# The first tile of a scan's coefficients normalised in four parts instead of two, under a newly searched written order

## Chip, cores and metric

One Trainium2 chip, one core. The time is microseconds (us) on the device for one execution of the program, from the host's data in the chip's main memory to the result there. Layout work on the host (permuting, padding, viewing the weights as 64-bit words) lies outside the time.

## What is computed

A gated linear attention with complex decay, and behind it one feed-forward layer (`moe`). Per batch, head and time step the decays are limited in magnitude, a 48x48 complex state is decayed and receives an outer product, and the query reads its real part:

```python
mag = np.sqrt(a_re * a_re + a_im * a_im)
scale = np.minimum(mag, 0.999) / (mag + 1e-06)
ar, ai = a_re * scale, a_im * scale            # "a normalised"
for t in range(768):                            # B=4, H=8, S=768, D=48
    new_re = ar[t] * S_re - ai[t] * S_im
    new_im = ar[t] * S_im + ai[t] * S_re
    S_re, S_im = new_re + outer(k[t], v[t]), new_im
    y[t] = q[t] @ S_re
h = y.reshape(3072, 384) @ w_in                 # 384 x 2048
out = (h * clip(h + 3, 0, 6) / 6) @ w_out       # 2048 x 384
```

## The kernel before

Time is cut into 24 chunks of 128 steps (`NCH`), each with a batch; two batches take turns. Three chunks at a time share one tile of coefficients: eight tiles, called q0 to q7 here, each with a `z` tile of 128 partitions x 2 (real, imaginary) x 18 rows x 68 columns, where the 18 rows are two halves `f` (time running backward and forward from the middle of a chunk) of nine rows.

The work is written as 13 streams, Python generators that each issue a few instructions between two `yield`s (a step). A string `ORDER` of letters says which stream makes its next step. The string is the program's order on every engine: TensorE (PE), VectorE (DVE), ScalarE (ACT), GpSimd (POOL) and the DMA queue of SyncE (SP) each run their own instructions strictly in the order in which they were written, and wait on one another by semaphores alone. The streams that matter here, with their letters:

- `load` (Z): one DMA of one part of a `z` tile. A tile is loaded into the place of the tile two before it, so q2's load waits until `prep` of chunk 2 has read q0 for the last time.
- `normal` (N for even, O for odd parts): normalises one part in four steps. Step 1 is ACT Square (its sum goes to a column of `accs`), an add of the two halves (DVE for q0, POOL for all later tiles) and ACT Ln; step 2 is two ACT Exp and a multiply (again DVE for q0, POOL later); step 3 one DVE instruction and an ACT Copy; step 4 one DVE instruction and the multiplication of the part itself (two DVE instructions of one plane each in half 0, one of both planes in half 1). Its scratch tile `sq` has two buffers, `y2` one. How a tile is cut into parts stands in `PARTS`: at most nine rows, so two parts for each tile.
- `chain` (C): running products over a whole tile on DVE, when all parts of it are normalised: seven steps, three steps e0 to e2 (written `pr`, `z`), six wide instructions of 882 elements, and at the end a few POOL instructions and six small DMAs (`cw`).
- `prep` (Q for chunk 1, P for the others): loads `u` and `gg`, then on ACT, DVE (POOL from q2 on) makes reciprocals of the products and multiplies q and k with them (`gg`, four products), and transposes through six DMAs `kq<-gg`; last a load of `vt`.
- `load_weights` (D) loads one of 16 blocks of both weight matrices (`ws`, four buffers); `weights` (W) turns the 64-bit words into numbers in two steps: ACT and one DVE instruction (L308), then two DVE, one ACT and one POOL instruction (L317).
- `mat` (A): the attention of one chunk: `pA` (PE), masked by DVE into `am`, `py`, transposes `pt` copied by ACT into `kn`, `pG` for the state, and the result `xh`, `xl`.
- `moe` (M): the feed-forward layer of three chunks at once, eight groups of 16 blocks: `ph` (PE), `r` (ACT), `hs` (DVE; from group 3 on `gh` and `gl`), `po` (PE). A group starts when its three chunks' `mat` steps are done.
- `weights_guard` (G), `wsplit` (S), `verdict` (V): checks of the weights' range, the splitting of `w_out` in two, and the final check of the inputs' ranges.

In the order before, the letters begin `ZNNZZZONQNOOOCNCCCCOCCCCCCOCCPDWPODDDWPQ`. Spelled out, with qT.i for part i of tile qT, up to the first feed-forward block:

```
load q0.0; normal q0.0 steps 1, 2; load q0.1, q1.0, q1.1; normal q0.1, q0.0, chunk 1's u, gg ... ;
chain q0 step 1; normal q1.0 step 1; chain q0 steps 2 to 5; normal q1.1 step 1; chain steps 6 .. e2, wide;
normal q1.1 step 2 (amid the wide ones); loads: chunk 0's u, gg, ws 0 to 3; weights 0; prep 0 (its six kq DMAs); ...
mat 0; weights 4, 5; (amid it) mat 1 pA; normal q1.0 steps 3, 4; weights 6 first step; prep 2 last products;
ws 7, 8, 9; weights 6, 7; prep 2 kq (3 DMAs); load q2.0; prep 2 kq (3); chain q1 step 1; ... weights 8;
normal q2.0 step 1; mat 1 py; load q2.1; mat 1 pt; vt of chunk 2; ws 10, 11; ... mat 1 pG, x; mat 2; moe block 0
```

## Time and profile before

| what | value |
|---|---|
| three runs | 712.55, 715.45, 721.03 us (median 715.45) |
| the profiled execution | 718.27 us, span of its instructions 716.5 us |
| PE busy | 593.6 us, 83% of the span |
| DVE busy | 510.7 us, 71% |
| ACT, POOL busy | 352.5 us, 175.9 us |
| granted TensorE clock, mean | 0.975 |

The 1.8 us between the span and the execution's time lie outside the first and last instruction. Busy PE is matmul time as modelled; the weight loads (PEld) overlap it. L12 is line 12 of the kernel.

Of the kernel before, what the change touches and what calls it, by code (L numbers as in the profile page):

```python
# [29 lines left out]

PAR = dict(
    PV=2, SZ='33333333', CS='3.3.3.3.3.3.3.3', GGB=1, SQB=2, ZB=2, XB=2, WTB=4, LAG=1, RB=2, OV=1, KQB=2,
    GS=3, VTB=2, IL=2
)

ORDER = (
    "ZNNZZZONQNOOOCNCCCCOCCCCCCOCCPDWPODDDWPQPPPPPPWWQWQWDQQQQPOANAPPWDAAACDWAAWWAAWNWNWPDDDWWPZPCWWCNAZA"
    "APDDWCWAAADACOAAACAACCACAMMCWMMMDCMMMMMCCCMMMWPMMMMMMMMMMMMPWPPMMMMMMMMWMDMMCMMWPPWMMMMMOWWPPMMMMMMM"
    "NMMMMOMWWMMMMDMMMAMMAMMPPMMMMANAAAPWPPMMPWNWMMMOPPPAAMMMMMMMMMMMMACPCMMMPGCPCGPGGGCCCCCMCMMMMMMMMPAA"
    "MGGZZCCCPAAAACOMMMMMMMMPPPMAAAMMMMMPPNAAAPPAPAAANMONAAPOMPMNMMMMMMOPMAAPMGMMMMMCMMMMPMMGPMMGGAAAACCC"  # L40
    "MMCPCMMMMMCCCGAMMMGMMMMPPPPGGAPPPMSSCAMMMMMMMAMMAMMMMGMMMMCCPCMGMAAPAAMMPPPPMMMMMMGMAMGMMMPMZZAAMMMM"
    "MMCNNPPAMAMMOMNMMAPOPMPMMMMMOMNOAMAMMMMMMPMMMMGMMMMMMMMMMAGAPCMMMMMPPCPAAAMMACMMMAACAACCCCMMGPMMMMMA"
    "MMPPPMMGGPGAMPPCCCMMMMMMMMMMMZAMAMASSCCNMMMMMMGNMMMPSMMPPSMMAPMMMMMPMASMSMMZGNSMPMMMMPPMMOMNAMSSMMMM"
    "MMPAASSSAOPMMMMMMAASPMMMMMPPMSAPAAAGPPPPPSMMMOMMOCMMMMMMMMMACCMMSSSSAMMMSSSMMMMMMCMPPMMMMGMCAMMPCPSG"
    "GAPMMCAMAMMAMMMZCPMCMMMMMCCPPPAAAMAACNNMMMMMMMMSMMMMMMMAAMMMMMMCCMMMMZPAMMMMMMMMMMMAMMMMAMMMMAMSPPMP"
    "MPOMMMSAAAMMMMPMPMMSMMMCMMMMMMMMOMMMMMMMMPPOANAMMSSMMMMMMMPMMPPMPPAOAAMMMAMSMMMMMMMMMAMNMMMMMPPMMMCA"
    "MPCMMMMAAACCMMMMMMMMMMMPMMMAPAAMMMMMMPMMMAMMMMCMMMMMMMMMMMMZCMMMMMMMMPCMCMNPCCMMMMMMMNMMAAAAMMMMAMPC"
    "MMMMMMZMAAAAMNCMCMMMPMMMMAMAPMMMMMMMCMPMMMMPPPPMMMMMAMMMMMMMMMMMMMMNOMOMMMPMMMMMAPAPMMMMMMMMAMMAMMMM"
    "MOMAMMPAMPAOPPPPPMMMMMMMMMAMMMMCCMMMMMPCCMMMMMMMAMAAMMMMMMMMMMMPPCMMMMMPPMMMMACAAAMMMCMMMMMCMAMMMMMM"
    "PMMMCCAAMAMCMMMMMMMMMGMAMMMPMAAACACPCMAPAMMMMPMMMMMMMMPPMPPMMMMMMMMMMMMMMMMMMMMMPAPMMMMMMMMAAMPPMMMM"  # L50
    "MMMMMMMMMMMMMAAMAMAMMMMMPMPPPMMMMMMMMMMMMMMMMMMMMMMMMMMMAMAPPPMMMMMMMMMMMMPMMMMMMMMMMMMMMMMPAAMMPMPM"
    "MAMMMMMMMMMMMMMMMPMMAAAMMMMMMMMMPAAAMMMMMMMMMMMMMMMMMAAMMMAAMMMMMMMMMMMMMMMMMMMMMMMMMMMMMMMMMMMMMMMM"
    "MMMMMMMMMMMMMMMMMMMMMVMMMMMMMMMMMMMMMMMMMMMMMMMMMMMMMMMMMMMMMMMMMMMMMMMMMMMMMMMMMMMMMMMMMMMMMMMMMVMM"
    "MM"
)
GGB, SQB, ZB, XB, WTB, LAG, RB, OV, KQB = (
    int(PAR[k]) for k in ("GGB", "SQB", "ZB", "XB", "WTB", "LAG", "RB", "OV", "KQB")
# [1 line left out]

GS, VTB = int(PAR["GS"]), int(PAR["VTB"])  # L60
PV = int(PAR.get("PV", 0))
# [2 lines left out]
SIZES = [int(x) for x in PAR.get("SZ", "222333333")]  # L64
NG, NCH = len(SIZES), B * S // C

IL, SEQ = int(PAR["IL"]), S // C
TURN = [(b + i) * SEQ + j for b in range(0, B, IL) for j in range(SEQ) for i in range(IL)]
FIRST = [sum(SIZES[:g]) for g in range(NG + 1)]
# [2 lines left out]
CHAINS, CHUNK, LAST = [], [], []  # L72
for _t, _ns in enumerate(PAR.get("CS", "3.3.3.3.3.3.3.3").split(".")):
# [3 lines left out]
    LAST.append(len(CHUNK) - 1)  # L77

PARTS = [
    [(f, x, min(9, 3 * n - x)) for f in range(2) for x in range(0, 3 * n, 9)] for _, n, _ in CHAINS  # L80
]
COLS = [sum(len(p) for p in PARTS[:q]) for q in range(len(CHAINS) + 1)]
MAXN = max(n for _, n, _ in CHAINS)
# [147 lines left out]
def tile_gated_attention_moe(ctx, tc, aL, GL, vL, wL, maskL, qkvaL, out):  # L231
# [66 lines left out]
    def weights(f):  # L298
# [10 lines left out]
        yield  # L309
        wout[f] = wp.tile([C, DM], F32, tag="wo", name="wo", bufs=NFF + (GS < NG))  # L310
        for part, bits in ((0, low[:, 0]), (1, wout[f].bitcast(I32))):
# [340 lines left out]
    def moe(g):  # L652
# [12 lines left out]

        split = g >= GS

# [57 lines left out]
    def wsplit(f):  # L725


        if "wl" not in LATE:
# [4 lines left out]
            LATE["wl"] = pl.tile([C, NFF, DM], F32R, name="wout_l")  # L733
        while f and GS and (GS - 1, f - 1) not in SECOND:
            yield "wait"
# [7 lines left out]
    def verdict():  # L743

        while len(NORMAL) < COLS[-1] or len(CWs) < len(CHAINS) or len(GUARDED) < 2 * NFF or "pg" not in LATE:
            yield "wait"
        ok = wp.tile([C, 8], F32, name="ok")
        P.memset(ok, 1.0)
        one = LATE["pg"].tile([C, DM], F32, tag="r", name="one", bufs=RB)
        for col, src, lim, op in (  # L750
            (0, accs[:, 0], SUM_M2_MAX, ALU.is_le),
            (1, accs[:, 1], SUM_Y_MAX, ALU.is_le),
            (2, n64, N64_MIN, ALU.is_ge),
            (3, wacc.rearrange("p a x -> p (a x)"), 1.0, ALU.is_le),
        ):
            p, n = src.shape
            t = one[:p, :n]
            V.tensor_scalar(t, src, lim, None, op)
            V.tensor_reduce(ok[:p, col : col + 1], t, mybir.AxisListType.X, ALU.min)
        okm = wp.tile([C, 1], F32, name="okm")  # L760
        V.tensor_reduce(okm, ok, mybir.AxisListType.X, ALU.min)
        yield
        pt = ps_a.tile([1, C], F32, tag="ps", name="pok")
        T.transpose(pt, okm, ident)
        okr = wp.tile([1, 1], F32, name="okr")
        V.tensor_reduce(okr, pt, mybir.AxisListType.X, ALU.min)
        V.tensor_copy(oki, okr)
        yield

    def each(make, items):  # L770
        for x in items:
            yield from make(*x)
# [15 lines left out]
        "D": each(load_weights, steps),  # L788
        "S": each(wsplit, steps if GS < NG else []),
        "V": verdict(),  # L790
# [117 lines left out]
```

### The profile page before, as it was taken

To read this page: it belongs to the slowest core of one execution; us is meant where nothing else is said; L and a number is where in the kernel's file an instruction comes from. 1 tells how busy PE (TensorE), PEld (TensorE's weight loads), DVE (VectorE), ACT (ScalarE), POOL (GpSimd) and SP (SyncE) were. 2 spreads that over 40 slices of the span, in tenths; PEclk is the share of its full clock that TensorE was granted. 3 is DMA by queue.
4 is the path that set the end of the run, shared out by engine and by line. 5 is a ranking of instruction groups with operands and counts; after the bars stand their busy time and mean duration, and the time that the engine had idled before them with its cause. 6 is when DMAs were issued, how large, how long until landed. Compare 5 with 4: busy or idle time off the path is not lost.

```text
span 716.5 us, 12111 instructions
## 1 busy us (share of the span) xinstructions
PE 593.6 (83%) x4433; PEld 521.7 (73%) x4433; DVE 510.7 (71%) x995; ACT 352.5 (49%) x721; POOL 175.9 (25%) x193
## 2 busy tenths in 40 slices
PE   0005359998568989989998999999999999999995
PEld 0004347776356767777777999999999998998995
DVE  3998857989858876787888657987688855453432
ACT  5334332565657776567646454444643443423332
POOL 0204230342143143315740333221302211300000
PEclk9999999999689999999999999999999999999998
DMA  9009872257746885476566234242453244140001
GB/s 344 23 18 206 253 211 78 67 121 163 183 102 161 194 225 96 127 179 157 104 126 150 80 72 79 86 70 90 82 126 45 82 82 78 50 60 34 1 0 38
DMA packets 55508, 79.61 MB, mean 111 GB/s; under 512 B 12432, under 2 KB 40208, under 8 KB 55440
## 3 DMA queue, kind: packets, MB, share of 16 engines
q1 hardware_dynamic: 55440, 78.75, 46.7%
q8 instruction: 37, 0.61, 0.4%
q14 instruction: 31, 0.25, 0.1%
HBM read 51.05 MB, written 4.72 MB: 78 GB/s over the span
## 4 chain that ended last, share of the span: by engine, by line
PE 38%; DMA 9%; DVE 8%; ACT 7%; issue 3%; POOL 3%; SPq 1%; ACTq 0%; DVEq 0%; POOLq 0%
PE ph L690 15%; PE po L673 5%; PE po L674 5%; PE po L675 5%; DMA kq<-gg 3%; PE py L585 3%; DMA out_dram<-ot 2%; DMA wgs<-in_wL_dram 2%; PE pA L569 2%; PE po L677 2%; PE pG L632 1%; ACT r L696 1%; DVE gg L528 1%; POOL gg L518 1%; DVE pr L408 1%
## 5 line engine op out<-in xcount | busy, mean ns | idle before, releaser
L696 ACT ACTIVATE r<-ph,half 128x384 f32<-128x384 f32 x128 | 73.7, 577 | 113.9 <-PE ph L690 109.4
L677 PE MATMUL po<-wo,hs 128*128 128x384 f32 x288 | 108.3, 509 | 16.7 <-DVE hs L708 16.7
L690 PE MATMUL ph<-xh,win_l 128*128 128x384 f32 x384 | 102.7, 376 | 2.8 <-ACT xh L647 2.8
L569 PE MATMUL pA<-kq 96*128 96x128 f32 x384 | 53.9, 296 | 61.2 <-DMA kq<-gg 59.3
L569 PEld LDWEIGHTS pA<-kq 96*128 96x128 f32 x384 | 51.7, 209 | 63.8 <-issue 61.4
L690 PE MATMUL ph<-xl,win_h 128*128 128x384 f32 x384 | 90.5, 344 | 1.0 <-DVE xl L648 1.0
L690 PE MATMUL ph<-xh,win_h 128*128 128x384 f32 x384 | 89.9, 342 | 0.0
L699 DVE SCALAR_TENSOR_TENSOR ph<-r,ph 128x384 f32<-128x384 f32 x80 | 44.8, 560 | 62.5 <-ACT r L696 62.3
L673 PE MATMUL po<-wh,gl 128*128 128x384 f32 x240 | 84.9, 354 | 4.2 <-DVE gl L704 3.8
L677 PEld LDWEIGHTS po<-wo,hs 128*128 128x128 f32 x288 | 53.9, 197 | 44.6 <-DVE hs L708 18.5
L674 PE MATMUL po<-wout_l,gh 128*128 128x384 f32 x240 | 81.9, 341 | 0.0
L675 PE MATMUL po<-wh,gh 128*128 128x384 f32 x240 | 81.0, 337 | 0.0
L690 PEld LDWEIGHTS ph<-xh,win_l 128*128 128x128 f32 x384 | 70.4, 192 | 14.4 <-ACT xh L647 2.9
L704 DVE TENSOR_TENSOR gl<-ph,gh 128x384 fp32r<-128x384 f32 x80 | 44.5, 557 | 41.0 <-ACT gh L702 40.9
L690 PEld LDWEIGHTS ph<-xl,win_h 128*128 128x128 f32 x384 | 69.4, 191 | 1.9 <-DVE xl L648 1.5
L690 PEld LDWEIGHTS ph<-xh,win_h 128*128 128x128 f32 x384 | 69.5, 190 | 0.6 <-issue 0.6
L702 ACT ACTIVATE gh<-ph 128x384 fp32r<-128x384 f32 x80 | 39.2, 490 | 60.9 <-DVE ph L699 60.9
L408 DVE TENSOR_TENSOR pr<-z 128x288 f32<-128x288 f32 (+2 forms) x176 | 66.6, 419 | 1.4
L518 POOL TENSOR_TENSOR gg<-gg,u 128x384 f32<-128x384 f32 x18 | 19.5, 1084 | 142.4 <-ACT u L516 126.7
L632 PE MATMUL pG<-vt,kn 128*96 128x64 f32 x320 | 34.9, 268 | 21.4 <-ACT kn L604 21.4
L673 PEld LDWEIGHTS po<-wh,gl 128*128 128x128 f32 x240 | 45.5, 189 | 8.4 <-DVE gl L704 7.3
L632 PEld LDWEIGHTS pG<-vt,kn 128*96 128x96 f32 x320 | 33.3, 183 | 24.6 <-ACT kn L604 22.1
(101 smaller groups left out, 1042.9 us busy)
## 6 DMA issues: line engine op xcount, KB each, us to landing
kq<-gg SPq DMA_DIRECT2D x138, 128.0 KB, 4.7
ws<-in_wL_dram SPq DMA_DIRECT2D x16, 768.0 KB, 7.2
wgs<-in_wL_dram SPq DMA_DIRECT2D x32, 384.0 KB, 3.8
z<-in_aL_dram SPq DMA_DIRECT2D x16, 612.0 KB, 5.5
vt<-in_vL_dram SPq DMA_DIRECT2D x24, 256.0 KB, 5.2
out_dram<-ot SPq DMA_DIRECT2D x24, 192.0 KB, 1.9
u<-in_GL_dram SPq DMA_DIRECT2D x23, 192.0 KB, 5.0
gg<-in_GL_dram SPq DMA_DIRECT2D x23, 192.0 KB, 2.6
```

The source lines that it names most:

```text
L408: V.tensor_tensor(pr[:, j], src, fac[:, j : j + 1].to_broadcast([C, *shape]), ALU.mult)
L569: T.matmul(pA[:, i], kt[:, hf * 4 + i], qt[:, hf * 4 + i], start=True, stop=True)
L632: T.matmul(pG[:, n], kn[:, n], vt[:, n], start=True, stop=True)
L673: T.matmul(po[i], gl[:, ts], wout_h[f], start=f == 0, stop=False)
L674: T.matmul(po[i], gh[:, ts], LATE["wl"][:, f], start=False, stop=False)
L675: T.matmul(po[i], gh[:, ts], wout_h[f], start=False, stop=f == NFF - 1)
L677: T.matmul(po[i], hs[0][:, ts], wout[f], start=f == 0, stop=f == NFF - 1)
L690: T.matmul(ph, w[:, f, kt * C : (kt + 1) * C], xx[:, kt], start=k == 0, stop=k == 8)
L696: A.activation(r, ph, AF.Relu, scale=1.0 / 6.0, bias=half)
L699: V.scalar_tensor_tensor(ph, r, 1.0, ph, ALU.min, ALU.mult)
L702: A.activation(gh, ph, AF.Copy)
L704: V.tensor_tensor(gl, ph, gh, ALU.subtract)
```

## The change

`PARTS` cuts tile q0 into parts of at most `R0` = 5 rows: per half one of five and one of four rows, four parts in place of two of nine (q1 to q7 keep nine). `accs` has 18 columns in place of 16, `load` makes 18 DMAs in place of 16, and `normal` has 18 parts in place of 16. The formulas, the tile of q0 and all else are the same. `ORDER` is a new string of 1,712 letters in place of 1,702.

```diff
 PAR = dict(
     PV=2, SZ='33333333', CS='3.3.3.3.3.3.3.3', GGB=1, SQB=2, ZB=2, XB=2, WTB=4, LAG=1, RB=2, OV=1, KQB=2,
-    GS=3, VTB=2, IL=2
+    GS=3, VTB=2, IL=2, R0=5
 )
 ORDER = (
-    "ZNNZZZONQNOOOCNCCCCOCCCCCCOCCPDWPODDDWPQPPPPPPWWQWQWDQQQQPOANAPPWDAAACDWAAWWAAWNWNWPDDDWWPZPCWWCNAZA"
-    "APDDWCWAAADACOAAACAACCACAMMCWMMMDCMMMMMCCCMMMWPMMMMMMMMMMMMPWPPMMMMMMMMWMDMMCMMWPPWMMMMMOWWPPMMMMMMM"
...
+    "ZZZZZNNZONNONOONONNDDDQOOPDOCCCCCCCCCCCCCWOOPWOPWPQPPPPWPQQWDDQNQWODANAWPQAAACWPAAPWWPWNZZWNWDDAANDW"
+    "CWCQWCWAPPAAWCPPAAADDAAOCWAAAADCCCAACWMMMMMCMMMMMCCDMMMMMMMMMMCMWMMPMMMMWPWDMMMMMMMMMMMMMMMCWWPPPMMM"
...
 )
+R0 = int(PAR["R0"])
 PARTS = [
-    [(f, x, min(9, 3 * n - x)) for f in range(2) for x in range(0, 3 * n, 9)] for _, n, _ in CHAINS
+    [(f, x, min(r, 3 * n - x)) for f in range(2) for x in range(0, 3 * n, r)]
+    for t, n, _ in CHAINS
+    for r in [9 if t else R0]
 ]
```

The new order spelled out up to the first feed-forward block:

```
load q0.0 to q0.3, q1.0; normal q0.0 steps 1, 2; load q1.1; normal q0.1 step 1, q0.0 steps 3, 4, q0.1 step 2,
q0.2 step 1, q0.1 steps 3, 4, q0.2 step 2, q0.3 step 1, q0.2 steps 3, 4; ws 0, 1, 2; chunk 1's u, gg;
q0.3 step 2, 3; chunk 0's u, gg; ws 3; q0.3 step 4; chain q0 whole (no other step amid it);
weights 0; normal q1.1 steps 1, 2; prep 0; normal q1.1 step 3; weights 1 first step; prep 0's products and kq DMAs; ...
prep 1's products; normal q1.0 step 1; ... mat 0 (py, pt, pG, x); prep 2 third step; weights 4; prep 2 last products;
weights 5; normal q1.0 step 3; load q2.0, q2.1; normal q1.0 step 4; weights 6; ws 7, 8; mat 1 pA; normal q2.0 step 1;
ws 9; chain q1 step 1; weights 7; vt of chunk 1; chain q1 steps 2, 3; mat 1 py; prep 2 kq (6 DMAs); mat 1 pt;
weights 8; chain q1 step 4; vt of chunk 2; mat 1 pG, x; ws 10, 11; mat 2 (weights 9 and chain q1 steps 5 to e1 amid it);
moe block 0
```

In the order before, chunk 1's vt is loaded ahead of mat 0. Between the first feed-forward block and the start of group 1 the two orders make nearly the same steps, in a somewhat different sequence. Of tile q3's chain, steps 2 to 6 stood between the `hs` of blocks 3 and 4 of group 1; in the new order steps 2 and 3 stand between the `hs` of blocks 2 and 3, steps 4 and 5 between those of 3 and 4, steps 6, 7, e0 and e1 between those of 4 and 5. The first step of `verdict` stands 11 steps from the end (81 before).

## Rows read from the trace of the kernel before

**Rows 1.** The page, part 1: busy time, share of the span, instructions per engine.

```profile
PE 593.6 (83%) x4433; PEld 521.7 (73%) x4433; DVE 510.7 (71%) x995; ACT 352.5 (49%) x721; POOL 175.9 (25%) x193
```

**Rows 2.** Busy time per stretch: stretch, length, PE PEld DVE ACT POOL, PEclk, DMA share, GB/s.

```profile
0.00:20.34 20.34, 0.00 (x0) 0.00 (x0) 8.68 (x12) 10.81 (x17) 1.46 (x11) 1.00 0.85 323
20.34:43.34 23.00, 0.00 (x0) 0.00 (x0) 22.17 (x50) 5.66 (x9) 4.02 (x3) 1.00 0.00 0
43.34:59.30 15.96, 0.00 (x0) 0.00 (x0) 15.62 (x27) 7.17 (x14) 3.34 (x3) 1.00 0.49 74
59.30:83.00 23.70, 17.41 (x128) 14.49 (x128) 20.03 (x31) 10.61 (x19) 8.74 (x14) 1.00 0.93 254
83.00:114.07 31.07, 15.67 (x123) 13.24 (x123) 19.50 (x47) 10.49 (x18) 7.74 (x6) 1.00 0.62 166
114.07:217.99 103.92, 82.82 (x549) 64.45 (x550) 84.44 (x159) 55.86 (x115) 31.61 (x34) 0.90 0.55 127
217.99:716.50 498.51, 477.68 (x3633) 429.51 (x3633) 340.22 (x674) 251.92 (x530) 118.99 (x124) 0.98 0.43 95
```

**Rows 3.** Timeline: start us, us, engine, line, operation, [idle before <-releaser]; PE's first work.

```profile
59.34 2.90 PE L569 MATMUL pA<-kq 96*128 96x128 f32 x12 [59.34 <-DMA kq<-gg]
...
114.67 1.33 PE L690 MATMUL ph<-xl,win_h 128*128 128x384 f32 x3 [1.03 <-DVE xl L648]
```

**Rows 4.** Timeline, 64 to 100 us: loads on SP's queue, and who waits.

```profile
64.00 0.59 SPq L551 DMA_DIRECT2D vt<-in_vL_dram  x1
...
74.95 5.22 SPq L295 DMA_DIRECT2D ws<-in_wL_dram  x3
...
84.49 0.55 SPq L357 DMA_DIRECT2D z<-in_aL_dram  x1
...
93.49 1.16 ACT L373 ACTIVATE sq<-z 128x1152 f32<-128x1152 f32 x1 [4.45 <-DMA z<-in_aL_dram]
...
97.45 2.82 PE L632 MATMUL pG<-vt,kn 128*96 128x64 f32 x16 [18.62 <-ACT kn L604]
...
99.10 1.03 DVE L308 SCALAR_TENSOR_TENSOR ws<-ws 128x768 int32<-128x768 int32 x1 [5.41 <-issue]
```

**Rows 5.** Waits of PE, 110 to 700 us: in total, times, longest.

```profile
PE po L677 <- DVE hs L708: 16.7, 6, 10.1
```

**Rows 6.** Tile z on SP's queue, first 20 us: its four loads, issue to landing.

```profile
DMA to landing us min/median/max: 4.4/6.2/7.9
```

**Rows 7.** Timeline, 5 to 45 us: instructions of normal's parts, and narrower ones.

```profile
5.61 1.16 ACT L373 ACTIVATE sq<-z 128x1152 f32<-128x1152 f32 x1 [3.59 <-DMA z<-in_aL_dram]
...
6.90 0.76 DVE L376 TENSOR_TENSOR sq<-sq 128x576 f32<-128x576 f32 x1 [6.90 <-ACT sq L373]
7.75 0.77 ACT L377 ACTIVATE sq<-sq,tiny 128x576 f32<-128x576 f32 x1 [0.89 <-DVE sq L376]
...
10.20 1.15 ACT L373 ACTIVATE sq<-z 128x1152 f32<-128x1152 f32 x1
...
44.21 0.55 DVE L518 TENSOR_TENSOR gg<-gg,u 128x384 f32<-128x384 f32 x1
```

**Rows 8.** Timeline, 19 to 27 us: POOL's first addition and DVE's chain beside POOL.

```profile
19.34 2.21 POOL L376 TENSOR_TENSOR sq<-sq 128x576 f32<-128x576 f32 x1 [18.35 <-ACT sq L373]
20.34 1.90 DVE L408 TENSOR_TENSOR pr<-z 128x288 f32<-128x288 f32 x2
...
22.83 0.83 DVE L408 TENSOR_TENSOR pr<-z 128x288 f32<-128x288 f32 x2
...
26.83 2.01 DVE L408 TENSOR_TENSOR pr<-z 128x288 f32<-128x288 f32 x2
```

**Rows 9.** Waits of DVE, 43 to 115 us: in total, times, longest.

```profile
DVE state L635 <- PE pG L632: 2.1, 1, 2.1
...
DVE ws L308 <- ACT ws L307: 1.9, 2, 1.0
```

**Rows 10.** DMA, 80 to 95 us: packets, bytes, rate.

```profile
DMA packets 1711, 3.33 MB, mean 222 GB/s; under 512 B 167, under 2 KB 935, under 8 KB 1711
```

More of the change, by code (lines that the diff above doesn't have):

```diff
@@ L32 @@
     PV=2, SZ='33333333', CS='3.3.3.3.3.3.3.3', GGB=1, SQB=2, ZB=2, XB=2, WTB=4, LAG=1, RB=2, OV=1, KQB=2,
-    GS=3, VTB=2, IL=2
+    GS=3, VTB=2, IL=2, R0=5
 )
 ORDER = (
-    "ZNNZZZONQNOOOCNCCCCOCCCCCCOCCPDWPODDDWPQPPPPPPWWQWQWDQQQQPOANAPPWDAAACDWAAWWAAWNWNWPDDDWWPZPCWWCNAZA"
-    "APDDWCWAAADACOAAACAACCACAMMCWMMMDCMMMMMCCCMMMWPMMMMMMMMMMMMPWPPMMMMMMMMWMDMMCMMWPPWMMMMMOWWPPMMMMMMM"
-    "NMMMMOMWWMMMMDMMMAMMAMMPPMMMMANAAAPWPPMMPWNWMMMOPPPAAMMMMMMMMMMMMACPCMMMPGCPCGPGGGCCCCCMCMMMMMMMMPAA"
-    "MGGZZCCCPAAAACOMMMMMMMMPPPMAAAMMMMMPPNAAAPPAPAAANMONAAPOMPMNMMMMMMOPMAAPMGMMMMMCMMMMPMMGPMMGGAAAACCC"
@@ L41 @@
[L41 to L54, printed above, removed]
+    "ZZZZZNNZONNONOONONNDDDQOOPDOCCCCCCCCCCCCCWOOPWOPWPQPPPPWPQQWDDQNQWODANAWPQAAACWPAAPWWPWNZZWNWDDAANDW"
+    "CWCQWCWAPPAAWCPPAAADDAAOCWAAAADCCCAACWMMMMMCMMMMMCCDMMMMMMMMMMCMWMMPMMMMWPWDMMMMMMMMMMMMMMMCWWPPPMMM"
@@ new lines @@
+    "MMNOWMMMPWOMWWMMMMMDMMMMMMMMPAAPPMAAMMMANAPWPPPPPMMPMWNWMOMMMAAMMMMMMMMMMMMCPCGCPCPCMMMPCCCCMCGAAAGG"
+    "GMMMMMMPMMGGAAZCZAMMMPAMCPCCOPMMMPMMAAAMPMMMPMMAAPNAPPAAANONAAAMMMPPMOMNMOMAPMMMMMAPPPMMMMCGMGAACAAM"
+    "MGCMMMMMMCGMMMMCPMMMMMCMCCCGGPMAMMMMMMMMPPPGGAPPPSCMAAMMMMMMMASGMMMMMMPCCAGCAAAMMPPMMMPMPPPMMGGZPAZA"
+    "MAACMMMNMMMMNMMMMMAMMAPONMPNMAPMMMMOOMOPMAMMMMMPAMMMGMMMMMMMMMMAMPGGCMMMMMMMMPPPCAAMAMMCACMMMMMAAAAA"
+    "PCCCMMPCPMMPMMMMMGPGGPAPCZZCMCMMMMMMMMMMMMSAMASNAMGCPPPCMMMMMMPNAMMMMMMAMMMMSPMSMNPASMSSMMMMSPGSSPAA"
@@ new lines @@
+    "APPPMMMMPMMONMMMMMMMMSSMMAOMMMMMMMAPMPGAPPMMPPASSSOAMOCMMMMMMMMMSAMMCCPMMMMPCMCMPMPPAAAGMMGPZMMMMMMA"
+    "AMMMMMMMMMMPMSMCCCAAMMMMPSMMMSACMPACCAMAANNCSMMMMMMAMMSMMMMMSMASMGSZMMMCMSMMMMMMPMSCMMMMMPMMMMMMMAAM"
+    "MASAPMPMOMMMAPPMOSMMMMMMMMAMNOMMMMMMMMMMMMMMMMMOMMMMSPAMCMPPPMMMMMMMMAAMMMMMMMPPMPPPPPNMAAAMMAMMMMMC"
+    "MSMMMMMMMMAAACPAMMMACMMMMMMMMMMMMMMMPMAPAMPPPZCPPMMMMMMMMMCAAMMMMMMMMMMMMCMMMMMMMMACCMCNMCMAMNMMMMMM"
+    "AAMMCMMMZMMMAMMMMMMCMCMAAAAPMMMMMMMAMAMMPMMMMPMMCMMNPMMMMMMMMMMMMMMMMMOMMMMNMPPMMMMMMMMAAAOMMPPPMMMM"
@@ new lines @@
+    "MMMMMAAAAMOMPMPPMMMMOAPPPMMMMMMMMMMAMMMCCAMCMMMMMMMMMMMMMACAPPMMMMMMMMMMMMMMMMPPCMAMMAPPAMMMMMMMPMMM"
+    "MCPACMMMMMMMMMCCACMMMMMMMMAAAMMAMGMAACACCMMMMAMMMMMCPMMAPMPMPPMMMMMMMMPPPAAPMMMMMMMMMMMMMMMMMMMMMMMM"
+    "MMAAMMMPMMMPAMMMMMMMMMAAMMAMMMMMMMMMPMPMAAMMMMMMMMMMMMMMMMMMMMMMMMMMMMMMMMAPPPPAAMMPMMMMMMAMMMMMMMMM"
+    "MMMPPMMMMMMMMPMPMMAMMPPMMMMMMMMMAMMMMMMMMMMMMMMMMMMMMMMMMMMMMMMAAAMMMAAAMMMAMMMMMMMMMMMMMMMMMMMMMMMM"
+    "MMMMMMMMMMMMMMMMMMMMMMMMMMMMMMMMMMMMMMMMMMMMMMMMMMMMMMMMMMMMMMMMMMMMMMMMMMMMMMMMMMMMMMMMMMMMMMMMMMMM"
@@ L55 @@
+    "MVMMMMMMMMMV"
 )
```

## The prediction

> **What bounds the kernel now.** The page's busy times come first: TensorE is busy for 83% of the span and VectorE for 71% [rows 1], so neither bounds the whole. The table by stretches shows why [rows 2]. TensorE does nothing until 59.3 us; VectorE is nearly full from 20.34 to 59.30 (37.8 of 39.0 us), so the first tile's chain and the first prep set the pace. From 59.3 to 114 TensorE is busy for 33 of 55 us. From 114 to 218 it idles 21.1 us; from 218 on it is busy 96%, and there its own work is the bound. So a microsecond saved ahead of the first feed-forward work (114.67, [rows 3]) counts in full if the stage to 218 only slides forward, and work added to VectorE after 218 costs little.
>
> The timeline between 64 and 100 us shows the largest single loss there [rows 4]. Three weight loads were issued from 74.95 on, the z load of tile q2 only at 84.49. ScalarE sits at that tile's Square until 93.49, 9.0 us after the issue, 4.45 of them idle. Behind it in ScalarE's order stand the kn copies and the weights' conversions, so TensorE's pG has waited 18.62 us at 97.45 and VectorE 5.41 us at 99.10. The reader is to see one late DMA stopping three engines. The waits of TensorE later on are short but for one: 16.7 us for hs in six waits, the longest 10.1 [rows 5].
>
> **The change part by part.** All terms are in the profiled execution's time, 718.27 us (span 716.5 and 1.77 around it); it lies 2.8 above the median of the runs.
>
> *Smaller first load.* The first part has 5/9 of 627 KB, so 279 KB fewer precede its end; at the first stretch's 323 GB/s [rows 2] that is 0.86 us. The whole part took 4.4 us to land [rows 6]. Bounds: 0 if latency alone counted, 2.0 (4/9 of 4.4) if all scaled. I take 0.86: the queue streams in this stretch. The Trainium skill ("DMA: Bandwidth & Descriptors", Anatomy of one DMA) gives for a GpSimd-issued load 2.0 us and bytes at 436 GB/s; by that, an estimate, 0.64 would be saved. The whole part would land in 3.4 by it against the 4.4 measured, so the trace decides.
>
> *Four parts in a row.* Before, the second part's Square follows the first's by 4.59 us (5.61, 10.20), and the chain starts 14.73 us after the first Square (20.34) [rows 7, 8]: one period and 10.14 us for the last part. Instructions don't shrink with the rows: DVE takes 0.76 us for 576 elements and 0.55 for 384, so 0.14 fixed, giving 0.49 for five rows and 0.42 for four. ACT takes 1.16 us for 1152 and 0.77 for 576, so about 0.38 fixed: 0.60 and 0.55, the Squares 0.81 and 0.73. The first period loses 0.35 (Square), 0.27 (add) and 3 x 0.17 (Ln, two Exp): 3.46. The next two also hold the previous part's Copy and come to about 3.4 and 3.7. The last part, four rows, of which the seven dependent steps Square, add, Ln, Exp, multiply, Copy and product all shrink by a quarter to a half, takes about 6.0. Sum 16.5, so 1.8 us more. Bounds: 11.6 if everything scaled with rows (14/9 x 4.59 + 4/9 x 10.14), a gain of 3.1; 23.9 if nothing did. I stay with 16.5, since it uses the slope of the same instructions.
>
> *POOL beside the chain.* In the old chain three POOL instructions of tile q1 each stretch one DVE group: 1.90 and 2.01 against 0.83, so about 1.1 us a time (the second POOL one falls between them) [rows 8]. The new order writes only q1.1's two beside it; ScalarE reaches them while the chain runs. One hit fewer: -1.1. It returns after the chain, when q1.0 is done: +1.1 (bounds 0 and 1.1).
>
> So the chain ends at -0.86 + 1.8 - 1.1 = -0.2: the four parts by themselves earn nothing.
>
> *Weights 1 ahead of prep 0's products:* one L308 instruction, 1.03 us [rows 4], delays the first kq DMAs, and the first pA goes from 59.3 [rows 3] to about 60.1. Chunk 0's attention then slides, but mat 1 has slack there (its pG is the one that waited 18.62).
>
> *Tile q2's load earlier.* It waits for the last products of prep 2, written now ahead of weights 5, the end of normal q1.0 and weights 6, together about 6 us of DVE work (two L308 at 1.0, two narrower ones of weights 5 at 0.55, four of normal at 0.76). It also goes ahead of the three ws loads. With the wait for kq DMAs and ws issues ahead of it on SP gone, issue at about 77.5 instead of 84.49, landing by the first stretch's 4.4 to 6.2 us at 82 to 84 instead of 93.5. DVE's idle time of 5.41 goes, and with it two waits of together 1.9 for ScalarE's conversions just before [rows 9]: idle time from 59.3 to 114.07 is 15.2 us [rows 2], of which 7.3 lie here. What is late next: two of prep 2's products no longer fill the wait for mat 0's pG (2 x 0.55 = 1.1), weights 7 waits for ScalarE behind q2.0's Square, POOL's add and Ln (about 1.4 by their sum), and mat 2's pA for kq DMAs that now stand behind vt (about 0.8). Net -7.3 + 1.1 + 1.4 + 0.8 = -4.0. Bounds: 0 (all of it re-appears) and -7.3. Two more steps, e0 and weights 9's end, come ahead of the first block; e0 (about 1.0, a narrower chain step) lies in the 2.1 us that VectorE waits for mat 2's pG [rows 9], so nothing; without that cover it costs 1.0.
>
> *SP's queue:* two more z loads, 0.5 us each to issue, at the front, where nothing waits for SP. The vt load of chunk 1 is moved past q2's loads and three ws; see the rivals. The verdict moves to the tail of DVE, which has no more feed-forward work there, two columns wider: nothing.
>
> Sum: -0.2 + 1.1 - 4.0 = -3.1 us at the first feed-forward block. From 114 to 717 TensorE idles 21.1 + 20.8 us before; steps are shuffled there, I take it as unchanged. 718.27 - 3.1 = 715.2; against the median 715.45 - 3.1 = 712.3, I say **712**.
>
> **The rivals.** *A, the moved vt is late (slower).* Before, chunk 1's vt was issued at 64.00 [rows 4], long before mat 1. Now two z, three ws (3.6 MB) and vt (0.26) must pass from 77.5 on, and ScalarE's kn of mat 1 needs the py that needs vt. At 400 GB/s it lands at 88 and hides behind weights 7 and 8, which hold ScalarE until about 92. It decides if the rate falls under 3.87 MB / 14.5 us = 267 GB/s. The stretch from 80 to 95 moved 222 [rows 10], the one from 59 to 83 254 [rows 2]; against it, those were full of kq's small packets, which now come behind. At 222 vt lands near 96 and pG starts at about 100 instead of 97.45, and prep 2's kq, 0.77 MB behind vt, lands 3.5 later still: +2.5 to +6 on the old time, 718 to 721. Chance 0.15.
>
> *B, the middle gets smoother (faster).* Between hs of blocks 3 and 4 of group 1, five chain steps of tile q3 stood before; now two. Besides the longest, the waits for hs are 6.6 us in five [rows 5]; if these go, and with them a third of what half clock costs after 218 (clock 0.98 on the mean: 4% of 498 us, 20 us, at 1.2 instead of 2.4 GHz [rows 2], so 10 us), it is 712 - 6.6 - 3 = about 703; for half of it 707. For it: the chain steps are spread out. Against: that is one place, and elsewhere steps are as bunched as before. Chance 0.23 for 702 to 708.
>
> *C, the gain is given back before 218.* The 10.1 us wait for hs comes from tile q2's whole chain written ahead of one hs, and it stays so in the new order. If group 1's start hangs on something that the start doesn't move (a load on SP behind others), the 21.1 us of idle time only grow: 715.5, +-2. For it: the stage has spare time. Against: VectorE is busy 84 of 104 us there, a queue that starts earlier should end earlier. Chance 0.2.
>
> **How the numbers follow.** Forecast 0.42 (709 to 716), C 0.2, B 0.23, A 0.15. Bounds of the terms reach from -7.3 - 2.9 to about +6, so 705 to 721; I cut at 705 and 719, leaving out half of A's upper end and the lower part of B. A difference under 1% (7.2 us; the three runs differ by 8.5) can't be told from none. Faster by over 1%, under 708.3: most of B and a bit of the forecast, 0.25; slower, over 722.6: the worse part of A and unforeseen waits, 0.1; within, 0.65.
>
> **What would show it.** Right: the chain of q0 starts at 20.5 to 22 and ends within 1 us of 43.4; the z load of q2 issued near 77 and ScalarE's Square at 82 to 85; VectorE's 5.41 us wait gone; the first block's second matmuls at 110 to 113 instead of 114.67; group 1 earlier by as much. Wrong: a chain that starts before 19 (fixed costs too high), PE waiting for vt in mat 1 (A), a first block earlier with group 1 unmoved (C), or the difference arising after 218 (B).

## The result and the profile after

The changed kernel took 711.62 us (median of 20 runs, 706.81 to 719.29) against 717.35 us of the kernel before in the same comparison: ratio 0.9921, 95% interval 0.9896 to 0.9946. Two later comparisons of the same kernel gave 0.9951 (0.9918 to 0.9984; 711.66 us) and 0.9931 (0.9900 to 0.9962; 711.19 us). It is faster by 3.5 to 5.7 us, 0.5 to 0.8%, inside the band that the prediction called "within 1%". The forecast was 712, 3.1 us faster.

The one execution of the first comparison that has a trace is a slow one, 717.59 us (span 715.8). The same kernel was profiled again in the last comparison at 711.9 us (span 710.1); it is called the second trace here. Line numbers are three higher than before up to the end of the file.

The page, part 1, of the first trace, beside [rows 1]:

```profile
PE 593.2 (83%) x4433; PEld 521.1 (73%) x4433; DVE 515.5 (72%) x1006; ACT 352.9 (49%) x735; POOL 178.1 (25%) x193
```

TensorE has the same work. VectorE has 11 instructions more, those of the two added parts, and 4.8 us.

The first tile's part of the first trace, 4 to 27 us, to set beside [rows 7, 8]:

```profile
4.36 0.74 ACT L376 ACTIVATE sq<-z 128x640 f32<-128x640 f32 x1 [2.33 <-DMA z<-in_aL_dram]
...
14.71 0.63 ACT L376 ACTIVATE sq<-z 128x512 f32<-128x512 f32 x1
...
20.72 0.83 DVE L411 TENSOR_TENSOR pr<-z 128x288 f32<-128x288 f32 x2
21.50 1.40 POOL L379 TENSOR_TENSOR sq<-sq 128x576 f32<-128x576 f32 x1 [20.50 <-ACT sq L376]
21.58 1.48 DVE L412 TENSOR_TENSOR z<-pr 128x144 f32<-128x144 f32 x1
...
24.18 0.31 DVE L412 TENSOR_TENSOR z<-pr 128x144 f32<-128x144 f32 x1
...
24.66 1.40 POOL L386 TENSOR_TENSOR sq<-sq,y 128x576 f32<-128x576 f32 x1 [1.76 <-ACT y L384]
24.74 2.00 DVE L411 TENSOR_TENSOR pr<-z 128x288 f32<-128x288 f32 x2
```

The chain starts 16.36 us after the first Square (14.73 before) and is hit by POOL twice instead of three times: 1.48 where the same instruction takes 0.31, 2.00 where the same two take 0.83. It ended at 42.75 us instead of 43.42. Its last instruction in the first trace, and below it that of the kernel before:

```profile
41.68 1.07 DVE L452 TENSOR_TENSOR z<-z,fx 128x882 f32<-128x882 f32 x1
42.35 1.07 DVE L449 TENSOR_TENSOR z<-z,fx 128x882 f32<-128x882 f32 x1
```

The stretch in which the prediction saw the largest loss, first trace, to set beside [rows 3, 4]:

```profile
77.76 1.07 SPq L360 DMA_DIRECT2D z<-in_aL_dram  x2
78.93 1.47 SPq L298 DMA_DIRECT2D ws<-in_wL_dram  x3
80.45 0.42 SPq L554 DMA_DIRECT2D vt<-in_vL_dram  x1
...
81.66 1.16 ACT L376 ACTIVATE sq<-z 128x1152 f32<-128x1152 f32 x1 [2.52 <-DMA z<-in_aL_dram]
...
93.09 1.94 PE L588 MATMUL py<-am,vt 128*32 128x128 f32 x32 [13.27 <-DMA vt<-in_vL_dram]
...
95.90 1.13 ACT L607 ACTIVATE kn<-pt 128x384 f32<-128x384 f32 x2 [4.62 <-PE pt L606]
...
96.44 1.86 PE L635 MATMUL pG<-vt,kn 128*96 128x64 f32 x10
...
112.41 1.33 PE L693 MATMUL ph<-xl,win_h 128*128 128x384 f32 x3 [0.18 <-DVE xl L651]
```

Tile q2's load leaves 6.7 us earlier and its Square starts 11.8 us earlier. TensorE still stands for 13.27 us in this place, now for chunk 1's `vt` at `py`; then `pG` follows without a wait. VectorE was relieved: from the first `pA` to the first block it idles 9.4 us, where it idled 15.2 before. Its largest wait from 43 to 112 us in the first trace, beside [rows 9] and the 5.41 us of [rows 4]:

```profile
DVE state L640 <- PE pG L635: 5.2, 2, 3.6
```

The stages, beside [rows 2]: length, busy time of PE, PEld, DVE, ACT, POOL, granted clock, DMA share, GB/s. First trace:

```profile
59.54:83.00 23.46, 13.84 (x88) 12.02 (x88) 20.94 (x31) 11.51 (x22) 10.49 (x15) 1.00 0.82 215
83.00:112.41 29.41, 18.95 (x163) 16.02 (x164) 22.57 (x50) 9.34 (x16) 8.14 (x6) 1.00 0.76 220
112.41:212.20 99.79, 82.60 (x550) 63.97 (x550) 81.26 (x157) 55.28 (x115) 31.73 (x34) 0.91 0.55 126
212.20:715.80 503.60, 477.86 (x3633) 429.04 (x3633) 342.94 (x674) 250.50 (x531) 120.56 (x124) 0.99 0.42 95
```

The second trace:

```profile
83.00:108.90 25.90, 18.95 (x164) 16.02 (x164) 21.19 (x49) 9.38 (x16) 6.72 (x5) 1.00 0.76 220
108.90:208.20 99.30, 83.30 (x550) 64.46 (x550) 81.23 (x157) 55.28 (x115) 31.10 (x34) 0.89 0.55 127
208.20:710.10 501.90, 479.02 (x3633) 429.85 (x3633) 343.86 (x674) 250.48 (x531) 120.00 (x124) 0.99 0.43 95
```

The stage up to group 1 in the kernel before, counted from its first block ([rows 2] counts from 114.07):

```profile
114.67:218.00 103.33, 82.83 (x550) 64.46 (x550) 83.86 (x157) 55.86 (x115) 31.61 (x34) 0.90 0.55 127
```

Two things are to be seen. The first block comes at 112.4 in one execution of this code and at 108.9 in another. And the stage from there to group 1 (103.3 us before) takes 99.8 and 99.3, with 81.2 us of VectorE's work in it instead of 83.9.

### The profile page after: what moved, and what is told of

The parts are those of the page before. It is cut to its first block, busy times and chain, and to the rows that moved or that the text cites. A ratio compares the mean times of both kernels' runs of the same rounds, so it can differ in the third digit from the quotient of the medians.

```text
span 715.8 us, 12152 instructions
## 1 busy us (share of the span) xinstructions
PE 593.2 (83%) x4433; PEld 521.1 (73%) x4433; DVE 515.5 (72%) x1006; ACT 352.9 (49%) x735; POOL 178.1 (25%) x193
## 4 chain that ended last, share of the span: by engine, by line
PE 34%; DVE 24%; DMA 16%; ACT 14%; issue 4%; POOL 4%; SPq 3%; DVEq 0%; ACTq 0%; POOLq 0%
PE ph L693 13%; PE po L676 4%; DVE pr L411 4%; PE po L677 4%; PE po L678 4%; DMA kq<-gg 4%; DMA wgs<-in_wL_dram 4%; DVE gg L531 3%; PE py L588 3%; PE pA L572 2%; ACT r L699 2%; PE pG L635 2%; DMA vt<-in_vL_dram 2%; DVE ph L702 2%; SPq L546 2%
## 5 line engine op out<-in xcount | busy, mean ns | idle before, releaser
L680 PE MATMUL po<-wo,hs 128*128 128x384 f32 x288 | 104.7, 497 | 10.6 <-DVE hs L711 10.6
L572 PE MATMUL pA<-kq 96*128 96x128 f32 x384 | 54.6, 297 | 66.3 <-DMA kq<-gg 60.1
L411 DVE TENSOR_TENSOR pr<-z 128x288 f32<-128x288 f32 (+2 forms) x176 | 69.4, 435 | 1.4
L588 PE MATMUL py<-am,vt 128*32 128x128 f32 x768 | 31.1, 305 | 26.9 <-DVE am L573 13.6
L531 DVE TENSOR_TENSOR gg<-u,z 128x384 f32<-128x384 f32 x92 | 51.5, 610 | 0.4
```

The lines of the kernel that those rows point to most:

```text
L411: V.tensor_tensor(pr[:, j], src, fac[:, j : j + 1].to_broadcast([C, *shape]), ALU.mult)
L531: V.tensor_tensor(gg[:, k, :, 1 - i].rearrange("p d (f s) -> p f d s", f=2), u[:, 2 * i : 2 * i + 2], zv[:, k], ALU.mult,)
L572: T.matmul(pA[:, i], kt[:, hf * 4 + i], qt[:, hf * 4 + i], start=True, stop=True)
L588: T.matmul(py[q * 32 : q * 32 + 32, t], lhs[:, n, cols], rhs, start=start, stop=stop, tile_position=(0, q * 32),)
L680: T.matmul(po[i], hs[0][:, ts], wout[f], start=f == 0, stop=f == NFF - 1)
```

## Experiments

Each ratio is to runs of the kernel before taken beside it (medians 716.56 us for the kernels e1 to e4, 714.74 for e5 to e8, 716.06 for e9 to e12). The kernels e5 and e12 are the changed kernel itself. Letters are counted in the order of the kernel named.

**The new start alone, the new rest alone.** Letter 372 of the new order and letter 362 of the old leave all streams at the same point, at the end of group 0, so the halves can be crossed.

```diff
 # e1_new_front, R0=5
-ORDER = new
+ORDER = new[:372] + old[362:]
 # e2_new_rest, R0=9
+ORDER = old[:362] + new[372:]
```

> The new order and the four parts up to the first blocks of feed-forward group 1 (372 letters), then the old order. Theory (the gain is made ahead of group 1, the rest of the new order is worth nothing): 5 to 6 us under before, ratio 0.991 to 0.994; group 1's last xl near 212 us. Rival (the gain lies in the smoother middle): within 2 us of before, ratio 0.997 to 1.003.

> The old order and two parts up to the first blocks of group 1, then the new order. Theory: within 2 us of before, ratio 0.997 to 1.003, the last xl of group 1 near 218 us. Rival (smoother middle): 4 to 6 us under before, ratio 0.991 to 0.995.

Measured: new start 0.9952 (0.9924 to 0.9981), new rest 0.9960 (0.9932 to 0.9988). Each alone is some 3 us faster, so "the rest is worth nothing" does not hold for the timed runs. What the traces say of it comes with the last experiments.

**Two parts under the new order; four under the old.**

```diff
 # e3_new_two_parts, R0=9
-ZZZZZNNZONNONOONONNDDDQOOPDO...
+ZZZNNZONNODDDQOPDO...
 # e7_old_four_parts, R0=5
-ZNNZZZONQNOOO...
+ZZZZZNNZONNONOONONNQOOO...
```

> The new order with tile q0 in two parts of nine rows, all later steps as in the new order. Theory (four parts earn nothing by themselves; they add 1.6 us to the normalisation and take 1.2 off the first load): the chain of q0 starts at about 20.0 to 20.4 instead of 20.72, and the whole is the same as the changed kernel within 1 us, ratio to before 0.990 to 0.994. Rival (the four parts are the gain): the chain starts later than 21.5 and the time returns to before, ratio 0.997 to 1.002.

> The order before with tile q0 alone in four parts, normalised in the sequence of the new order. Theory (four parts cost 1.0 us at the chain's start): the chain starts near 20.7 to 21.4, the first pA at 59.9 to 60.4, the rest as before; ratio 1.000 to 1.003. Rival (the four parts help): the chain starts before 20.3, ratio under 0.998.

Measured: two parts under the new order 0.9899 (0.9872 to 0.9925; 710.11 us), four parts under the old 1.0017 (0.9985 to 1.0048). The four parts earn nothing, in either order: 0.9899 is no worse than any of the changed kernel's three ratios, though the two were not timed side by side. The trace of the old order with four parts shows why:

```profile
5.00 0.74 ACT L376 ACTIVATE sq<-z 128x640 f32<-128x640 f32 x1 [2.97 <-DMA z<-in_aL_dram]
...
21.35 2.03 DVE L411 TENSOR_TENSOR pr<-z 128x288 f32<-128x288 f32 x2
...
60.34 2.05 PE L572 MATMUL pA<-kq 96*128 96x128 f32 x8 [60.34 <-DMA kq<-gg]
```

The first Square to the chain is 16.35 us, as in the changed kernel, and the first `pA` comes 1.0 us later than in [rows 3]. Under the new order the chain ended at 41.49 and 41.70 us in the two traces with two parts and at 42.59 to 43.43 in the six with four.

**Chunk 1's vt early again (rival A).** Chunk 1's last `prep` step goes back to right behind its `kq`, ahead of tile q2's loads.

```diff
 # e4_new_vt_early and e11_vt_early_again, R0=5; e8 the same with two parts
-...ANAWPQAAACWPAAPWWPWNZZWNWDDAANDWCWCQWC...
+...ANAWPQQAAACWPAAPWWPWNZZWNWDDAANDWCWCWC...
```

> The changed kernel with one letter moved: chunk 1's vt is loaded right after its kq transfers, ahead of q2's loads. Theory (mat 1's py waits 13 us for vt and holds kn, pG and the first block): the wait goes, py of mat 1 runs near 83 instead of 93, the first block's second matmuls at 109 to 111 instead of 112.4; 1 to 3 us under the changed kernel, ratio to before 0.986 to 0.992. Rival (kq of chunk 2, 6.6 us of issues behind it, sets mat 2 anyway): first block still at 112 to 113, ratio 0.990 to 0.994.

> The new order with both mended: tile q0 in two parts and chunk 1's vt loaded right after its kq transfers. Theory (the 1.0 us of the four parts counts once vt no longer sets mat 1): first pA at 58.3, the first block's second matmuls at 107 to 108; 1.5 to 3 us under the changed kernel, ratio to before 0.985 to 0.990. Rival (the kq of chunk 2 sets mat 2 whatever comes earlier): the first block at 108.5 as with vt early alone, ratio 0.989 to 0.991.

> The changed kernel itself, once more, so that the others of this set are compared with it on one chip and its trace can be read a second time. Theory (the landing of chunk 1's vt differs from execution to execution, 90.0 to 93.1 us so far, and the first trace of it was a late one): vt lands at about 90 us, the first block's second matmuls at 109.5 and not 112.4; ratio to before 0.990 to 0.994. Rival (the changed order itself is later than the mixtures): 112 to 113 again.

Measured: 0.9898 (0.9869 to 0.9927; 709.75 us) with four parts, 0.9935 (0.9909 to 0.9962) with two parts, and 0.9951 for the changed kernel beside the latter. With two parts the first block came at 109.4 us, not at the 107 to 108 expected. In the changed kernel's trace `py` of mat 1 started at 91.9 us behind vt, and the first block still came at 108.8. The first number, 0.9898, looked like a gain, but had no run of the changed kernel beside it. So both ran again, side by side:

> The changed kernel with chunk 1's vt loaded ahead of tile q2's loads (as it ran once, 0.9898), now beside the changed kernel itself in the same call. If the late vt costs what the first run says: first block 1.5 to 3.5 us earlier than in the changed kernel's profile of this call, median 1.5 to 3 us lower, ratio 0.989 to 0.992. If the wait only moves to the next late thing (kn behind ScalarE's weights, then chunk 2's kq): median within 0.8 us of the changed kernel's.

> The changed kernel once more, as the partner of the run with vt early: ratio 0.992 to 0.995, median 710.5 to 712, py of mat 1 at 90 to 93 us behind vt. Seen as a sample: if its vt lands at 90 and not at 93, the first block comes 1.5 to 3 us earlier than in the first profile (112.41), which would say that the landing of this one load moves the start of the feed-forward work from one execution to the next.

Measured: 0.9940 (0.9905 to 0.9974; 710.62 us) with vt early, 0.9931 (0.9900 to 0.9962; 711.19 us) without: the same. With vt early (timeline, 83 to 96 us):

```profile
83.22 2.11 PE L588 MATMUL py<-am,vt 128*32 128x128 f32 x32 [3.29 <-DVE am L573]
...
92.16 0.86 ACT L607 ACTIVATE kn<-pt 128x384 f32<-128x384 f32 x2
...
92.70 2.82 PE L635 MATMUL pG<-vt,kn 128*96 128x64 f32 x16 [5.90 <-ACT kn L607]
```

The changed kernel, second trace:

```profile
89.58 1.94 PE L588 MATMUL py<-am,vt 128*32 128x128 f32 x32 [10.71 <-DMA vt<-in_vL_dram]
...
92.39 1.13 ACT L607 ACTIVATE kn<-pt 128x384 f32<-128x384 f32 x2 [2.48 <-PE pt L606]
92.93 2.82 PE L635 MATMUL pG<-vt,kn 128*96 128x64 f32 x16
```

`py` comes 6.4 us earlier and `pG` 0.2. In the changed kernel ScalarE has done its weights at 89.9 and idles 2.48 us for `pt`, which waits behind `py`; in the first trace it idles 4.62. With vt early it goes from the weights straight to the kn copies, but this execution reached them late: tile q2's Square had started at 82.9 instead of 79.9. Counted from that Square, the first block comes after 27.2, 26.7 and 28.2 us in the three traces with vt early, and after 30.8, 28.9, 26.6, 29.0 and 29.5 us in the five of the new start with vt late: 1.6 us less on the mean, with a scatter of 4. So most of the 10.71 us wait is hidden behind the weights, up to 4.6 us at `pG` are not, and what is left of that in the timed runs is too small for them to show.

**Only tile q2's load early, in the old order.**

```diff
 # e6_old_q2_early, R0=9
-...WNWPDDDWWPZPCWWCNAZAAPDDW...
+...WNWPZZDDDWWPPCWWCNAAAPDDW...
```

> The kernel before with one thing moved: tile q2's two loads are written right after prep 2's last products, ahead of the three weight loads. Theory (this load's lateness stopped ScalarE, TensorE and VectorE): ScalarE's Square of q2.0 at 88 to 90 instead of 93.5, mat 1's pG at 92 to 94 instead of 97.5, the first block's second matmuls at 110 to 112 instead of 114.7; ratio 0.994 to 0.998. Rival (the weights, now behind it, stop the same engines): the first block within 1 us of 114.7, ratio 0.998 to 1.003.

Measured: 1.0046 (1.0015 to 1.0076), slower. Timeline of it, 80 to 98 us:

```profile
80.36 1.02 DVE L531 TENSOR_TENSOR gg<-u,z 128x384 f32<-128x384 f32 x2
...
81.44 0.90 SPq L360 DMA_DIRECT2D z<-in_aL_dram  x2
82.43 1.50 SPq L298 DMA_DIRECT2D ws<-in_wL_dram  x3
88.60 0.88 ACT L310 ACTIVATE ws<-ws 128x768 int32<-128x768 uint32 x1 [6.17 <-DMA ws<-in_wL_dram]
...
93.50 1.15 ACT L376 ACTIVATE sq<-z 128x1152 f32<-128x1152 f32 x1
...
97.59 2.67 PE L635 MATMUL pG<-vt,kn 128*96 128x64 f32 x15 [20.29 <-ACT kn L607]
```

Two more views of it: SP's wait at the load (in total, times, longest), and the rate of the DMA from 75 to 95 us in slices of half a us.

```profile
SPq L360 <- DVE gg L531: 7.7, 1, 7.7
```

```profile
GB/s 25 20 0 0 0 0 0 0 0 0 0 0 0 0 24 201 274 362 411 406 401 409 472 406 418 418 393 406 430 320 332 270 270 307 272 281 135 168 168 145
```

The load left 3.1 us earlier than in [rows 4], and its first part landed after 3.6 us. But SP runs its instructions in order: it stood 7.7 us at this load, until VectorE had made prep 2's last products. The three weight loads, now behind it, left at 82.43 instead of 74.95, and from 76 to 82 us nothing was moved at all. ScalarE needs weights 7 before the Square, so Square and `pG` stand where [rows 4] has them. The load was early in the order; what it waits for was not. So this kernel does not test the prediction's term by itself. The new order writes prep 2's products ahead of weights 5 and 6 as well, so that the load leaves at 76.0 to 78.3 us, and it writes q2's Square ahead of weights 7 and 8. What each of the two is worth, no run shows.

**Where the rest's gain lies.** The old order with only group 1's letters new, and with only those of groups 2 and 3:

```diff
 # e9_old_group1_new, R0=9
+ORDER = old[:362] + new[372:545] + old[535:]
 # e10_old_groups23_new, R0=9
+ORDER = old[:535] + new[545:1019] + old[1009:]
```

> The order before, but letters 363 to 535 (from the end of group 0's feed-forward work to about block 12 of group 1, with tile q3's chain in it) are those of the new order; two parts. If the prediction's rival B has its place right (chain steps of q3 between the hs of blocks 3 and 4 of group 1), most of the gain of 'the old start, the new rest' (0.996) is here: ratio 0.995 to 0.998, the hs waits of group 1 shorter than the 2.2 us each of before, first ot of group 1 less than 75.5 us after the last xl of group 1. If the gain lies in groups 2 and 3, as the marks of the earlier runs have it: ratio 0.999 to 1.001, from the first ot of group 1 to that of group 3 again 159.5 to 160.5 us, and the 2.8 us wait of TensorE for kn near 385 still there.

> The order before, but letters 536 to 1009 (from about block 12 of group 1 to just before the first block of group 4) are those of the new order; two parts. If the rest's gain lies here: from the first ot of group 1 to that of group 3 155 to 157.5 us instead of 160.0, TensorE's 2.8 us wait for kn near 385 gone, ratio 0.995 to 0.997. If the gain lies in group 1 or after group 4: ratio 0.999 to 1.001 and the stretch again 159.5 to 160.5 us. If it needs the new order of group 1 as well (the two lean on each other), neither this run nor the one with group 1 alone shows more than a third of it.

Measured: 0.9988 (0.9957 to 1.0020) and 0.9981 (0.9944 to 1.0018): neither can be told from 1. The stretch from the first `ot` of group 1 to that of group 3 was 160.1 and 156.6 us, as the second theory had it, and TensorE's wait for kn is in the former only. With group 1 alone new (PE's timeline, 380 to 387 us):

```profile
380.24 1.57 PE L635 MATMUL pG<-vt,kn 128*96 128x64 f32 x16 [2.90 <-ACT kn L607]
...
383.98 0.52 PE L678 MATMUL po<-wh,gh 128*128 128x384 f32 x1
...
386.93 0.34 PE L676 MATMUL po<-wh,gl 128*128 128x384 f32 x1
```

But the mark was badly chosen. With groups 2 and 3 new, from the start of group 1 (its last `xl`) to that first `ot` took 79.2 us, against 76.1 with group 1 alone new and 75.9 before: the new order has more of the attention's steps ahead of the `ot` and fewer behind it. From the start of group 1 to the end of the span four traces with the old rest have 498.5 to 501.9 us, mean 500.3; seven with the new rest, without the first trace (503.6), 496.5 to 501.9, mean 499.9. The last piece, from group 4 on, did not run alone; from the first `ot` of group 3 to the end of the span six traces with its old letters have 262.5 to 265.2 us, mean 263.9, and these seven with the new ones 263.3 to 265.3, mean 264.2. The traces show no gain in the rest. The wait for kn goes, and waits for hs, gl and state grow. What the timed 0.9960 of the new rest is made of stays open; its interval reaches up to 0.9988, and the two middle pieces multiplied give 0.997, neither of them clear of 1.

## Why the prediction was right, and where by luck

These are the traces that have either start whole, with four parts (new) or two (old), the first block being the `ph` row of [rows 3]:

| start | trace | first block | group 1 starts |
|---|---|---|---|
| old | before | 114.7 | 218.0 |
| old | new rest | 112.6 | 214.3 |
| old | group 1 new | 109.1 | 209.5 |
| old | groups 2, 3 new | 109.1 | 210.7 |
| new | changed, first | 112.4 | 212.2 |
| new | new start | 109.5 | 209.8 |
| new | changed, again | 108.8 | 209.8 |
| new | changed, second | 108.9 | 208.2 |

The means are 111.4 and 213.1 for the old start, 109.9 and 210.0 for the new. So group 1 starts 3.1 us earlier, the forecast's sum to the tenth; four traces a side that spread over 8.5 and 4.0 us make that tenth an accident, and without the first trace it is 3.9 us, with 2.3 at the first block. In the timed runs the new start alone is 3.4 us faster and the whole 3.5 to 5.7. The sum also came together otherwise than predicted: 1.5 us are there at the first block, where 3.1 were expected, and 1.6 arise between it and group 1, where nothing was.

- *Smaller first load, 0.86:* the first Square starts at 4.22 to 5.05 us (seven traces, mean 4.57) with five rows and at 4.96 to 5.61 (seven, mean 5.18) with nine: 0.6. The row's value was a little high. The 4.4 us that the whole part took to land was the latest of seven traces; the others have 3.7 to 4.0. The Trainium skill ("DMA: Bandwidth & Descriptors", Anatomy of one DMA) had given 0.64 by estimate, and the traces agree with that.
- *Four parts in a row, 16.5 us:* 16.35 to 16.36 in seven traces. VectorE's slope and fixed part held (0.49 and 0.42 us). ScalarE's Squares took 0.74 and 0.63 us instead of 0.81 and 0.73: its line had been drawn through two different functions.
- *One POOL hit fewer, 1.1:* the chain from start to end takes 22.03 us instead of 23.08. Right. One hit made an instruction of 0.31 last 1.48, ending 0.16 us after POOL's own 1.40. The Trainium skill ("SBUF — State Buffer", SBUF: two separate sides) says that a GpSimd instruction that reads SBUF, the core's own memory, and a VectorE instruction with two inputs there lock each other out for a whole instruction; the rows agree. The hit returned as said, +1.1: in every trace with the new start one of chunk 1's four products takes 1.64 us instead of 0.55 beside POOL's addition for q1.0. The first trace, two products each:

```profile
54.59 2.10 DVE L531 TENSOR_TENSOR gge<-ue,z 128x384 f32<-128x384 f32 x2
...
57.49 1.02 DVE L531 TENSOR_TENSOR gge<-ue,z 128x384 f32<-128x384 f32 x2
```

- *Chain end −0.2:* 42.67 to 42.93 us (mean 42.8) against 42.93 to 43.42 (mean 43.1) in the traces of the table. Right, and with it that the four parts alone earn nothing: against two parts under the same order they end the chain some 1.2 us later.
- *Weights 1, first pA at 60.1:* 59.5 to 59.8 us (mean 59.6) against 58.9 to 59.3 (mean 59.1). Later by 0.6, where 0.8 was expected.
- *Load of q2 at 77.5, Square at 82 to 84, the 5.41 wait gone:* issued at 76.0 to 78.3, Square at 79.9 to 82.2, since the load landed after 3.7 to 3.9 us and not 4.4 to 6.2; the wait is gone. Right, and the Square even earlier.
- *Net −4.0 from it:* **this step failed in size.** The first block comes 1.5 us earlier on the mean of the table. The chain gave 0.3 of that, and POOL's returned hit took between 0 and 1.1 back. So of the 4.0 us between 1.2 and 2.3 are there (without the first trace 2.1 to 3.2). VectorE's idle time from the first `pA` to the first block, of which 7.3 us were to go, is 15.2, 13.6, 8.7 and 8.7 us in the four traces with the old start and 9.4, 6.3, 4.8 and 7.2 in the four with the new: 4.6 less on the mean, and 2.6 us more work stands there. The base of the term, the landing 9.0 us after the issue and ScalarE's 4.45 idle [rows 4], is of one execution. The same start in the trace with group 1 new:

```profile
82.67 0.55 SPq L360 DMA_DIRECT2D z<-in_aL_dram  x1
...
87.80 1.16 ACT L376 ACTIVATE sq<-z 128x1152 f32<-128x1152 f32 x1 [0.62 <-DMA z<-in_aL_dram]
...
109.12 1.33 PE L693 MATMUL ph<-xl,win_h 128*128 128x384 f32 x3 [1.03 <-DVE xl L651]
```

The load lands after 5.1 us, ScalarE idles 0.62, and the first block is as early as in the changed kernel's two later traces. As these eight traces have it, what the new order saves here is mostly what the transfers happen to lose in the old one: 2.3 us between the latest traces of each, 0.2 to 0.4 between the earliest.

- *From 114 to 717 unchanged:* **failed for the first part.** The forecast noted that weights 9's end and chain q1's e0 come ahead of the first block and priced them there at nothing, which fits: VectorE still waits 1.2 us for mat 2's `pG` behind e0 in three of the four traces (2.1 before). It missed what they leave behind: VectorE has 81.2 to 81.3 us of work up to group 1 in the four traces with the new start and 83.1 to 83.9 in the four with the old, in a stage that [rows 2] shows VectorE filling to four fifths. TensorE's waits over the stage fall from 19.4 to 21.5 us to 16.2 to 19.7. That these two steps are the cause is read from the rows; no kernel moved them alone. From group 1 on, "unchanged" holds in the traces; the timed 0.9960 of the new rest speaks against it and stays open.
- *Rival A:* its mechanism came, TensorE waits 10.7 to 13.3 us for vt. Its price did not: vt early gave 0.9940 beside 0.9931. The cover that the prediction named, ScalarE held by the weights, hides all but 2.5 to 4.6 us of it, and the new start is not later than the old for all that. Nor does the landing of this load by itself set the first block: with `py` at 89.6, 90.1, 91.9 and 93.1 us it came at 108.9, 109.5, 108.8 and 112.4.
- *Rival B:* the 702 to 708 us did not come, and the place was wrong. With q3's chain spread, the waits for hs beside the longest (6.6 us) did not go. TensorE's waits from 110 to 700 us in the second trace, beside [rows 5]:

```profile
PE py L588 <- DVE am L573: 13.1, 2, 9.4
PE po L680 <- DVE hs L711: 7.2, 9, 1.9
```

- *Rival C:* the long wait behind tile q2's chain stayed, as it said, 9.4 us now under the name of `am`; the gain was not given back before group 1.

## What to carry over

Before a wait is priced at what one trace shows, ask whether it ends on a transfer: such a wait moves by several us between executions of the same code (ScalarE's for tile q2 was 4.45 us in one and 0.62 in another), and the change is worth the mean of it, not the row. A load that goes first in a queue that runs in order holds all loads behind it until what it waits for is done; move that work ahead too. And steps that go ahead of a mark "for nothing" are work that a busy engine no longer has behind it.

## What was not expected of the chip

The rate of the DMA queue over the same 20 us differed between executions of the same code. The kernel before, 75 to 95 us:

```profile
DMA packets 2114, 5.03 MB, mean 251 GB/s; under 512 B 230, under 2 KB 998, under 8 KB 2114
```

The kernel with the same start and group 1 new:

```profile
DMA packets 2258, 5.96 MB, mean 298 GB/s; under 512 B 227, under 2 KB 995, under 8 KB 2257
```

At 251, 273, 298 and 299 GB/s the first block of the old start came at 114.7, 112.6, 109.1 and 109.1 us. TensorE's own work does not explain that: from 83 us to the first block it is busy 15.67 us in the latest of the four traces and in the earliest. What makes the rate differ, no run here shows.

Here a wait of TensorE cost more than its length. After the 2.90 us wait for kn the matmuls of `po` took 0.52 us each, and 0.34 from 386.4 on. The granted clock of that stretch was 0.72 in the mean, so part of it lay at the lower of the two levels, 1.2 instead of 2.4 GHz (columns as in the stages above; group 1 alone new):

```profile
380.20:384.30 4.10, 4.06 (x25) 4.06 (x26) 3.93 (x17) 2.39 (x5) 0.67 (x1) 0.72 1.16 151
```

With groups 2 and 3 new, and no such wait, the same place has:

```profile
379.00:383.00 4.00, 4.00 (x62) 3.37 (x60) 3.34 (x14) 3.64 (x8) 0.00 (x0) 1.00 1.05 149
```
